# Softmax row sums of two head pairs in one block, sent back through DRAM, and SBUF work moved to GpSimd, in a fused cosine attention and MLP kernel

## Chip, cores, metric

One core of one Trainium2 chip. The metric is the device time of one execution in microseconds (us), as the median of several; lower is better.

## The reference, cut to what matters

```python
# q, k, v: (8 batches, 12 heads, 448 tokens, 64) fp32; w_in: (768, 2048); w_out: (2048, 768); tau = 0.1
q_n = q / (np.linalg.norm(q, axis=-1, keepdims=True) + 1e-06)     # k_n likewise
scores = np.matmul(q_n, k_n.transpose(0, 1, 3, 2)) / tau
scores = scores - np.max(scores, axis=-1, keepdims=True)
attn = np.exp(scores)
attn = attn / (np.sum(attn, axis=-1, keepdims=True) + 1e-09)
x = np.matmul(attn, v)          # then heads side by side: (3584, 768)
h = x @ w_in
out = (0.5 * h * (1.0 + erf(h * inv_sqrt2))) @ w_out
```

## The kernel before

In the profile PE is TensorE, PEld its weight loads, DVE is VectorE, ACT ScalarE, POOL GpSimd and SP SyncE, which issues DMAs here; SPq is its queue. PSUM is the memory that TensorE's products go to, in banks; SBUF holds the other tiles on the chip. Twelve heads make six head pairs per batch (HP = 6). For each pair, q and k are scaled to length one and transposed (`tp`), the scores are computed transposed (`st`, keys on the partitions), and exp gives `pt`. Two products follow: `o` = values, and `sm` = row sums, by a matrix of ones 64 columns wide, so that each sum comes out 64 times, once beside each value of its head. x = o / sm. After six pairs, the first layer (`hp`, 16 chains of six matmuls) follows, then gelu. The second layer (`op`) runs as filling between the next batches' attention.

```python
    def scale(g):                      # a pair's q and k, scaled
        sr = sr_t.pop(g)               # the norm, from ScalarE: exp(0.5 * ln(sum of squares))
        se = nrm.tile(...)
        nc.vector.tensor_scalar(se, sr, 1e-6, None, ALU.add)
        rn = nrm.tile(...)
        nc.vector.reciprocal(rn, se)
        ...
        for i, eng in enumerate((nc.gpsimd, nc.vector)):      # one half on each engine
            eng.tensor_tensor(qkb[:, i]..., t[:, i], rn[:, i].to_broadcast(...), ALU.mult)

    def transposes(g):
        tp = ps_acc.tile([128, 2, NC, CS], BF16, tag="sm", name=f"tp{g}")   # the bank of the sums
        ...                                                   # 8 transposes
        nc.vector.tensor_copy(qkT, tp)

    def values(g):
        o = ps_acc.tile([128, 512], F32, tag="o", name=f"o{g}")
        sm = ps_acc.tile([128, 512], F32, tag="sm", name=f"sm{g}")
        for dst in (sm, o):
            for c in range(NC):
                for h in range(2):
                    nc.tensor.matmul(dst[h * D:(h + 1) * D, :S],
                                     lhsT=ones if dst is sm else v_t[g][:, h, c, :],
                                     rhs=pt_t[g, c][:, h, :], start=(c == 0), stop=(c == NC - 1))

    def normalise(g):
        ln = rcp.tile([128, S], F32, tag="ln", name=f"ln{g}")
        nc.scalar.activation(ln, sm[:, :S], AF.Ln)
        rs = rcp.tile([128, S], F32, tag="rs", name=f"rs{g}")
        nc.scalar.activation(rs, ln, AF.Exp, scale=-1.0)
        nc.vector.tensor_tensor(x_t[b][:, p, :], o[:, :S], rs, ALU.mult)
    # cut: loads, squares, reduce, root, scores, attention, first, second_pieces, spin (matmuls whose
    # result nobody reads, between the first batch's steps)
```

## Time and profile before

| | before |
|---|---|
| median of 3 runs | 488.82 us (488.04 to 489.09) |
| profiled span | 487.9 us |
| mean granted TensorE clock | 0.993 |
| first hp starts at | 49.88 us |
| batch with 128 op matmuls, hp start to hp start | 58.74 us |
| batch with 96 | 54.43 us |
| last hp start to the end | 43.90 us |

How to read it: the span is the first hp start, seven steps from hp start to hp start, and the last part. Three steps have 128 op matmuls; of the four with 96, one (the first) takes 54.74. The page's own lines are in the prediction. The granted clock by slices of 12.2 us: only the second slice is low.

```profile
PEclk9799999999999999999999999999999999999999
```

### The profile page before, as it was taken

The numbers are of one execution on the slowest core, as the hardware profiler recorded it, in microseconds if no ns is written. First come the engines' busy times: TensorE is split into PE (matmuls) and PEld (weight loads), VectorE is DVE, ScalarE is ACT, GpSimd is POOL, SyncE is SP. The second block draws the span as 40 slices with busy tenths as digits, with TensorE's granted clock in tenths as the row PEclk, the third lists the DMA queues.
The fourth block names the chain that finished last, engine by engine and source line by source line (L and its number), as shares of the span: only waits on it lengthen the run. The fifth ranks groups of instructions, "written<-read, shape, count | busy, mean of one in ns | idle before, by whom it ended". The sixth has DMA issues, their size and how long they took to land.

```text
span 487.9 us, 8097 instructions
## 1 busy us (share of the span) xinstructions
PE 474.8 (97%) x3280; PEld 245.2 (50%) x3280; DVE 198.5 (41%) x349; ACT 323.1 (66%) x530; POOL 195.8 (40%) x158
## 2 busy tenths in 40 slices
PE   7599999999999999999999999999999999999996
PEld 4254554455554555455545555455555555445563
DVE  4569116721366115650276213760166502631021
ACT  3498569954887448974688547975688646994400
POOL 5789306840367204860077402780066600610000
PEclk9799999999999999999999999999999999999999
DMA  9699964460165302461054500652045210221022
GB/s 216 141 203 233 234 105 115 108 159 1 28 166 142 80 1 80 117 158 29 0 128 131 156 2 6 171 130 76 0 119 137 52 32 1 53 44 32 1 61 68
DMA packets 42053, 45.35 MB, mean 93 GB/s; under 512 B 3360, under 2 KB 37664, under 8 KB 42016
## 3 DMA queue, kind: packets, MB, share of 16 engines
q1 hardware_dynamic: 27280, 32.81, 22.3%
q0 software_dynamic: 14496, 11.80, 16.1%
q8 instruction: 25, 0.41, 0.4%
q10 hardware_dynamic: 240, 0.23, 0.1%
q14 instruction: 12, 0.10, 0.1%
HBM read 45.61 MB, written 11.01 MB: 116 GB/s over the span
## 4 chain that ended last, share of the span: by engine, by line
PE 88%; DMA 4%; ACT 3%; DVE 2%; POOL 1%; issue 1%; SPq 1%; POOLq 0%
PE op L200 30%; PE hp L299 30%; PE st L161 10%; PE sm L174 7%; PE o L174 6%; PE tp L150 4%; DMA qk<-in_k_dram 4%; ACT pt L164 2%; PE spin L240 1%; DVE x L185 1%; POOL qkb L139 1%; SPq L89 1%; ACT rs L184 1%; DVE qkT L151 1%; ACT ln L182 0%
## 5 line engine op out<-in xcount | busy, mean ns | idle before, releaser
L164 ACT ACTIVATE pt<-st 112x896 bf16<-112x896 f32 x192 | 165.0, 911 | 29.7 <-PE st L161 27.8
L139 POOL TENSOR_TENSOR qkb<-qk,rn 112x512 bf16<-112x512 f32 x48 | 69.4, 1447 | 232.9 <-DVE rn L135 213.4
L200 PE MATMUL op<-wo,g 128*128 128x384 bf16 x896 | 161.3, 326 | 0.0
L299 PE MATMUL hp<-x,wi 128*128 128x448 bf16 x768 | 147.9, 352 | 0.1
L301 ACT ACTIVATE g<-hp 128x448 bf16<-128x448 f32 x128 | 69.6, 544 | 80.2 <-PE hp L299 80.2
L200 PEld LDWEIGHTS <-g 128*128 128x128 bf16 x896 | 81.2, 98 | 62.4 <-issue 15.9
L299 PEld LDWEIGHTS <-wi 128*128 128x128 bf16 x768 | 74.8, 98 | 68.8 <-issue 0.4
L110 POOL TENSOR_TENSOR sq<-qk 112x1024 f32<-112x1024 f32 x46 | 87.7, 1907 | 2.0 <-DMA qk<-in_k_dram 1.4
L151 DVE COPY qkT<-tp 128x896 bf16<-128x896 bf16 x48 | 29.7, 620 | 101.3 <-PE tp L150 101.3
L204 DVE COPY ot<-op 128x384 f32<-128x384 f32 x56 | 31.1, 555 | 92.1 <-PE op L200 92.0
L185 DVE TENSOR_TENSOR x<-o,rs 128x448 bf16<-128x448 f32 x48 | 30.0, 624 | 81.4 <-ACT rs L184 60.1
L161 PE MATMUL st<-qkT 64*112 64x448 bf16 x384 | 60.7, 376 | 1.6 <-DVE qkT L151 0.7
L119 DVE TENSOR_REDUCE nq<-sq 112x16 f32<-112x1024 f32 x47 | 56.9, 1211 | 1.8 <-POOL sq L110 1.8
L174 PE MATMUL sm<-pt,ones 112*64 112x448 bf16 x384 | 45.8, 360 | 0.0
L174 PE MATMUL o<-pt,v 112*64 112x448 bf16 x384 | 44.3, 352 | 0.0
L161 PEld LDWEIGHTS <-qkT 64*112 64x112 bf16 x384 | 20.5, 125 | 39.3 <-issue 28.1
L182 ACT ACTIVATE ln<-sm 128x448 f32<-128x448 f32 x48 | 25.5, 532 | 21.3 <-PE sm L174 21.2
L139 DVE TENSOR_TENSOR qkb<-qk,rn 112x512 bf16<-112x512 f32 x48 | 37.1, 773 | 1.9 <-DMA qk<-in_k_dram 0.2
L97 POOL DMA_DIRECT2D v<-in_v_dram x48 | 34.2, 712 | 0.2 <-issue 0.2
L150 PE MATMUL tp<-ident,qkb 112*128 112x112 bf16 x384 | 27.9, 215 | 5.3 <-DVE qkb L139 4.4
L150 PEld LDWEIGHTS <-qkb 112*128 112x128 bf16 x384 | 20.5, 98 | 20.7 <-issue 13.2
L174 PEld LDWEIGHTS <-ones 112*64 112x64 bf16 x384 | 17.7, 109 | 23.1 <-issue 15.9
(26 smaller groups left out, 162.7 us busy)
## 6 DMA issues: line engine op xcount, KB each, us to landing
qk<-in_q_dram SPq DMA_DIRECT2D x48, 224.0 KB, 2.8
qk<-in_k_dram SPq DMA_DIRECT2D x47, 224.0 KB, 3.8
v<-in_v_dram POOLq DMA_DIRECT2D x48, 112.0 KB, 3.6
wi<-in_moe_w_in_dram POOLq DMA_DIRECT2D x6, 512.0 KB, 10.3
wo<-in_moe_w_out_dram POOLq DMA_DIRECT2D x4, 768.0 KB, 18.9
out_dram<-ot SPq DMA_DIRECT2D x8, 336.0 KB, 3.8
out_dram<-ot SPq DMA_DIRECT2D x8, 288.0 KB, 3.8
out_dram<-ot SPq DMA_DIRECT2D x8, 240.0 KB, 3.2
```

The lines of the kernel that those rows point to most:

```text
L110: nc.gpsimd.tensor_tensor(sq, t, t, ALU.mult)
L119: nc.vector.tensor_reduce(nq, sq, mybir.AxisListType.X, ALU.add)
L139: eng.tensor_tensor(qkb[:, i].rearrange("p c h d -> p h c d"), t[:, i], rn[:, i].to_broadcast([CS, 2, NC, D]), ALU.mult)
L150: nc.tensor.transpose(tp[:, i, c, :], qkb[:, i, c].rearrange("p h d -> p (h d)"), ident)
L151: nc.vector.tensor_copy(qkT, tp)
L161: nc.tensor.matmul(st[:, h, :S], lhsT=qkT[rows, 1, c, :], rhs=qkT[rows, 0, :, :], start=True, stop=True)
L164: nc.scalar.activation(pt, st[:, :, :S], AF.Exp, scale=inv_tau)
L174: nc.tensor.matmul(dst[h * D:(h + 1) * D, :S], lhsT=ones if dst is sm else v_t[g][:, h, c, :], rhs=pt_t[g, c][:, h, :], start=(c == 0), st ...
L185: nc.vector.tensor_tensor(x_t[b][:, p, :], o[:, :S], rs, ALU.mult)
L200: nc.tensor.matmul(ps[:, :NH], lhsT=g_t[sb][:, kf, t * 128:(t + 1) * 128], rhs=wo[:, kf, ni * NH:(ni + 1) * NH], start=(kf == 0), stop=(kf ...
L299: nc.tensor.matmul(hp[:, :S], lhsT=wi[:, kd, m * 128:(m + 1) * 128], rhs=x_t[b][:, kd, :], start=(kd == 0), stop=(kd == KD - 1))
L301: nc.scalar.activation(g_t[sb][:, m, hf * S:(hf + 1) * S], hp[:, :S], AF.Gelu)
```

## The change

Its intent is to take work off TensorE, which bounds the kernel, and to keep VectorE and GpSimd out of each other's way. In each batch the row sums of pairs 0 and 1, and of 2 and 3, are computed in one block on four 32-column tiles. Such a sum stands in 32 rows and not beside its values, so one row of each head is stored to DRAM and read back broadcast over 64 partitions (`rb`); GpSimd then makes x from `rb` and from a copy of o in SBUF. GpSimd also takes both scalings; VectorE keeps what reads PSUM or has one operand. Norms of three pairs share a root. The weights are loaded in halves of columns, and the first four hp chains get their last matmul late.

```diff
+    rows = nc.dram_tensor("rows", (NG, 2, S), F32, kind="Internal").ap()
     def root(n):                       # now for a group of up to five pairs
+        se = nrm.tile(shape + [2], F32, tag="se", name=f"se{n}")[..., 0]     # output stride 2
+        nc.vector.tensor_scalar(se, sr, 1e-6, None, ALU.add)
+        rn = nrm.tile(shape, F32, tag="rn", name=f"rn{n}")
+        nc.vector.reciprocal(rn, se)
     def scale(g):
-        for i, eng in enumerate((nc.gpsimd, nc.vector)):
+        for i, eng in enumerate((nc.vector if g == 0 else nc.gpsimd, nc.gpsimd)):
+    def sums_two(g):
+        sm = ps_acc.tile([128, 512], F32, tag="sm", name=f"sm{g}")
+        for c in range(NC):
+            for j in range(2):
+                for h in range(2):
+                    r = 32 * (2 * j + h)
+                    nc.tensor.matmul(sm[r:r + 32, :S], lhsT=ones[:, :32], rhs=pt_t[g + j, c][:, h, :],
+                                     start=(c == 0), stop=(c == NC - 1), tile_position=(0, r))
+        rs = reciprocal(g, sm)
+        nc.sync.dma_start(out=rows[g:g + 2].rearrange("j h s -> (j h) s"), in_=rs[0:128:32, :])
+        rb = osp.tile([128, 2, S], F32, tag="rb", name=f"rb{g}", bufs=2)
+        for h in range(2):
+            nc.sync.dma_start(out=rb[h * D:(h + 1) * D], in_=rows[g:g + 2, h, :].partition_broadcast(D))
     # attention(b), step i, g = 6 * b + i:
+                values(g - 1, i < HP - 1)          # with a copy of o to SBUF by VectorE
+                if i in (2, 4):
+                    sums_two(g - 2)
...
+            upto(load_v, g + (3 if b == 0 else 4))
+            if i in (3, 5):
+                for j in (3, 2):
+                    normalise(g - j, nc.gpsimd)
     # first(b): chains 0 to 3 to their fifth matmul, then
+        for m in range(4):
+            mm(m, (KD - 1,))
     # prologue
-    upto("v", 3, load_v)
+    upto(load_v, 1)
+    upto(load_wi, 1)
 # cut: pools, weights by halves, reduce, spins, order of op
```

## The prediction

> **What bounds the kernel now.** I read the page first, then the timeline of TensorE in steady batches, then the first 52 us of all engines.
>
> ```profile
> PE 474.8 (97%) x3280; PEld 245.2 (50%) x3280; DVE 198.5 (41%) x349; ACT 323.1 (66%) x530; POOL 195.8 (40%) x158
> PE   7599999999999999999999999999999999999996
> L174 PE MATMUL sm<-pt,ones 112*64 112x448 bf16 x384 | 45.8, 360 | 0.0
> L174 PE MATMUL o<-pt,v 112*64 112x448 bf16 x384 | 44.3, 352 | 0.0
> ```
>
> TensorE is 97% busy and full in every slice but the first two and the last. Busy is not the same as at its peak, so I took starts of successive blocks in the timeline as the cost of a block. Here is one pair (two heads) in a batch with 128 op matmuls:
>
> ```profile
> 131.25 0.95 PE L174 MATMUL sm<-pt,ones 112*64 112x448 bf16 x8
> 132.03 0.92 PE L174 MATMUL o<-pt,v 112*64 112x448 bf16 x8
> 132.88 0.59 PE L161 MATMUL st<-qkT 64*112 64x448 bf16 x4
> 133.40 0.57 PE L150 MATMUL tp<-ident,qkb 112*128 112x112 bf16 x8
> 133.80 1.79 PE L200 MATMUL op<-wo,g 128*128 128x384 bf16 x10
> 135.52 0.58 PE L161 MATMUL st<-qkT 64*112 64x448 bf16 x4
> ```
>
> From start to start: sm 0.78 us, o 0.85, st 0.52, tp 0.40, op 1.72 for ten. In the trace's starts a plain op follows the last by 163 ns, an hp by 189 ns, and the two column halves of an sm start 3 or 4 ns apart, one such round each 189 ns. The last matmul before a change of array shape takes about 94 ns more (256 for 162, 283 for 189). There is nothing else: no waits. The starts of the eight first-layer (hp) stages are 49.88, 104.61, 163.35, 217.79, 276.53, 330.96, 389.70 and 444.01, so a batch with 96 op matmuls takes 54.4 us, one with 128 takes 58.7, and 43.9 us follow the last start. The 96-op batches have one blemish, scores that wait for ScalarE to free their buffer:
>
> ```profile
> 191.30 0.58 PE L161 MATMUL st<-qkT 64*112 64x448 bf16 x4
> 193.41 0.82 PE L161 MATMUL st<-qkT 64*112 64x448 bf16 x4
> ```
>
> Summed over a batch, st takes 7.02 us there and 6.25 in a 128-op batch: 0.77 us of waiting.
>
> The first batch, 49.9 us to its hp, is another matter. From 25 us on ScalarE sets the pace, one pair each 5.07 us (25.43, 30.50, 35.57, 40.64):
>
> ```profile
> 25.43 3.53 ACT L164 ACTIVATE pt<-st 112x896 bf16<-112x896 f32 x4
> 28.85 0.31 ACT L125 ACTIVATE lq<-nq,tiny 112x16 f32<-112x16 f32 x1
> 29.19 0.22 ACT L127 ACTIVATE sr<-lq 112x16 f32<-112x16 f32 x1
> 29.42 0.54 ACT L182 ACTIVATE ln<-sm 128x448 f32<-128x448 f32 x1
> 30.00 0.58 ACT L184 ACTIVATE rs<-ln 128x448 f32<-128x448 f32 x1
> ```
>
> GpSimd is nearly as full there, and it and VectorE get in each other's way when both work on two SBUF operands:
>
> ```profile
> 38.41 0.69 DVE L139 TENSOR_TENSOR qkb<-qk,rn 112x512 bf16<-112x512 f32 x1
> 38.55 1.46 POOL L139 TENSOR_TENSOR qkb<-qk,rn 112x512 bf16<-112x512 f32 x1 [0.50 <-DVE rn L135]
> 42.52 3.75 DVE L139 TENSOR_TENSOR qkb<-qk,rn 112x512 bf16<-112x512 f32 x1
> 44.06 1.05 POOL L139 TENSOR_TENSOR qkb<-qk,rn 112x512 bf16<-112x512 f32 x1
> ```
>
> GpSimd needs 1.05 us for a scaling when VectorE is held up, and 1.46 when it starts 0.14 us after VectorE's. So some 0.4 us of GpSimd's usual 1.45 is waiting, and VectorE's 3.75 is 0.69 of work and 3 of waiting.
>
> **What the Trainium skill says.** "SBUF — State Buffer", SBUF: two separate sides: VectorE with two SBUF inputs, or in a 2-port mode, and GpSimd share a port pair as an exclusive lock held for a whole instruction. The 1.05 against 1.46 and the 3.75 agree. "TensorE: Matmul & The Clock Gate", Part 3: Packing small matmuls: tiles in different column groups run together, about 4 ns apart, three of 32 columns giving 2.38 times. Two tiles agree here (3 to 4 ns); four are not in this trace. "TensorEngine Tiling (Array Packing)", Key Properties: changing the tiling mode drains the engine. The 94 ns agree. "DMA: Bandwidth & Descriptors", Anatomy of one DMA: about 2.0 us fixed per DMA, mostly the receipt of the write. The page's out_dram stores land in 3.2 to 3.8 us with 240 to 336 KB; nothing so small as the new row store is in the trace.
>
> **The change, part by part: steady batches.**
> - Row sums. Today 6 blocks of sm, 6 x 0.78 = 4.68 us. Afterwards two pairs keep theirs (1.56), and two blocks of 16 matmuls on four 32-column tiles serve the other four. If four run as two do, a block is four rounds of 189 ns and a little for the first weights, 0.80 (an estimate from the sm block). That is 3.16 in all: 1.52 saved.
> - The 64-column values now go into 32-column sums: one change of shape more for each block, 2 x 0.094 = 0.19 lost.
> - Sums and transposes share one PSUM bank. Before, o and st (1.37 us) stood between sm and tp, and hid ScalarE's ln, which frees it. Now only st (0.52) does. ln starts 0.394 us after the last sm matmul's start (so when nothing else holds ScalarE), 0.21 after the block's end, and takes 0.54; with 0.05 for the signal tp starts at 0.80, not 0.52: 0.28 lost, twice a batch, 0.56.
> - The first four hp chains run to their fifth matmul and only then get their sixth. The first gelu starts 20 x 0.189 = 3.78 into the stage plus 0.389 (the trace's distance from last matmul to gelu), ends at 4.72, and the fifth chain, due at 24 x 0.189 = 4.54, needs its buffer: 0.25 lost.
> - ScalarE loses two ln/rs couples (2.2 us) and four ln/exp root couples (2 us) a batch. In 128-op batches this is beside TensorE. In 96-op batches it ends the 0.77 of waiting, but behind a shared sum the four exps still come late (end 2.95 us after it, second st at 2.78): 0.23 twice, so 0.77 - 0.46 = 0.31 won.
> - VectorE's 32 copies of o, GpSimd's 48 more scalings and 32 products, and 16 broadcasts of 448 KB lie beside TensorE: GpSimd would do 12 x 1.05 + 6 x 1.9 + 6 x 0.71 + 4 x 0.9 = 32 us of a 54 us batch.
> - The round trip: rs at 1.35 us after the shared sum, a row store about 2.5 (fixed cost and issue), a broadcast about 4.5 (3.8 to land as a qk load, plus a second issue), two products 1.8: 10.2. TensorE reaches the hp that needs them after about 11.4 in the shortest batch. Hidden, with 1.2 us to spare.
>
> Sum: 128-op batch -1.52 + 0.19 + 0.56 + 0.25 = -0.5, so 58.2; 96-op batch 0.31 better, -0.8, so 53.6.
>
> **The first batch.** GpSimd takes both scalings, so its load per pair is 2 x 1.05 + 1.9 (squares) + 0.71 (v) + about 0.6 (weights) = 5.3 us, above ScalarE's 3.53 + 0.53 + on average 0.73 = 4.8. Followed in order from the scaling of pair 1 at 12.8 us: pairs 2, 3, 4 and 5 are scaled by about 20.8, 26.1, 31.4 and 38 (two products before the last, perhaps waiting for the broadcast). From a scaling to the first exp go 1.5 us (tp 0.4, copy 0.6, st), and the last pair needs 4.7 on ScalarE and 1.7 of sums and values: hp at about 46. The v loads of pairs 1 and 2 queue behind a 1.5 MB weight load in a phase where DMA is full (v takes 7.7 us to land in the first 75 us); one us for that: 47. Today it is 49.9, and hp then waits 0.3 for its last x. Gain 3.2. Loading wo only after this stage costs nothing by this working: at the pace of the software queue (11.8 MB in 16.1% of 488 us, 150 GB/s written) the first two column halves, 1.57 MB, need 10.5 us, and hp takes 18. The five-pair root group at the end of that stage delays a transpose by 0.35.
>
> **Sum.** 47.0 + (53.6 + 0.35) + 3 x 58.2 + 3 x 53.6 + 43.9 + 0.25 = 480.5 us of span against 487.9: 7.4 less. On the median, 481.4; I say 481.
>
> **Rivals.**
> - The packing alone decides and the new waits do not appear: ln is prompt or the bank is not the thing waited for. Then 8 x 1.5 + 3 + 4 us go, 469 to 473. For it: TensorE is the bound, all it sheds counts. Against: the order of waits of the built kernel shows tp after each shared sum waiting for ScalarE.
> - The round trip is not hidden: row stores queue behind qk loads and output stores on the same queue, and hp waits 1 to 3 us in seven batches. 485 to 500. For it: 1.2 us to spare. Against: DMA is only 30% busy in steady batches.
> - GpSimd becomes the bound of the first batch: its scalings stay at 1.45, 0.8 us a pair more over five pairs, hp at 51: 485. Against: the 1.05 with VectorE held up.
> - Four tiles run no better than two pairs of tiles: no saving, 493. Against: rounds of 189 ns leave room for eight instructions at the 49 ns that a transpose and its weight load take together.
>
> **Range and chances.** The start may be off by 3 us either way, a steady batch by 0.5 us, seven times: 475 to 487. The 2% line is 479.0, two us below my number: faster 0.32, same 0.64, slower 0.04.
>
> **What would show it.** A shared sum of 16 with 0.75 to 0.85 from start to start; tp after it with a wait of about 0.3 on ScalarE's ln; hp stages 58.2 and 53.6 apart; the fifth hp chain 0.25 late; GpSimd's scalings near 1.05; first hp at 45 to 49. Wrong if x products of GpSimd end hp's wait, if PE is throttled in the first batch, or if op waits for wo in the second.

## The result, and the profile after

| | before | after | predicted |
|---|---|---|---|
| median | 488.71 us (488.04 to 489.09, 4 runs) | 488.58 us (488.36 to 488.73, 4 runs) | 481.0 |
| ratio | | 0.9998 (0.9981 to 1.0016) | |
| span profiled | 487.9 | 486.7 | 480.5 |
| first hp starts at | 49.88 | 54.38 | 47.0 |
| first step (96 op, to the second hp) | 54.74 | 54.04 | 53.95 |
| step with 128 op, three times | 58.74 | 58.05 | 58.2 |
| step with 96 op, three times | 54.43 | 53.35 | 53.6 |
| last hp start to the end | 43.90 | 44.04 | 44.15 |

A ratio here is the mean time of one kernel's fast runs over the mean of the other's in the same rounds, with a 95% interval, so it is not quite the ratio of the medians quoted. The time is the same, and it is outside the range that I gave.

The columns tell where it went. From the second hp on, the changed kernel is 5.75 us faster (0.70 + 3 x 0.69 + 3.12 - 0.14; the three 96-op steps before are 54.43, 54.43 and 54.31). It gives 4.50 of that back before the first hp, and the span is 1.2 us shorter. (The medians are only 0.1 apart: the profiled execution of before took 489.69 us, 1 us over its median.) My steady batches were right to a quarter of a us each. My first hp was 7.4 us too early.

The page first: busy time, the slices and the three groups that matter.

```profile
PE 465.0 (96%) x3266; PEld 235.5 (48%) x3266; DVE 164.7 (34%) x246; ACT 297.5 (61%) x443; POOL 254.8 (52%) x234
PE   8586999999999999999999999999999999999996
PEclk9978999999999999999999999999999999999998
L151 POOL TENSOR_TENSOR qkb<-qk,rn 112x512 bf16<-112x512 f32 x95 | 97.2, 1048 | 92.8 <-PE op L244 72.2
L230 POOL TENSOR_TENSOR x<-os,rb 128x448 bf16<-128x448 f32 x32 | 35.5, 1126 | 93.3 <-DMA rb<-rows 77.0
L140 DVE TENSOR_SCALAR se<-sr 112x48 f32<-112x48 f32 (+2 forms) x20 | 8.4, 419 | 78.3 <-ACT sr L137 78.3
```

VectorE's load fell as intended, and GpSimd's scaling takes 1048 ns against 1447 before. But the PE row now has four slices under 9 at its start, and the clock row is low in the third and fourth: the loss is before 49 us. Note too the mean of 419 ns for the small add: by the trace its median is 191, so a few were very long.

The steady batch, on TensorE's timeline (start, duration, engine, line, operation, tiles, count):

```profile
140.57 0.95 PE L183 MATMUL o<-pt,v 112*64 112x448 bf16 x8
141.45 0.94 PE L216 MATMUL sm<-pt,ones 112*32 112x448 bf16 x16
142.32 0.58 PE L173 MATMUL st<-qkT 64*112 64x448 bf16 x4
143.03 0.55 PE L162 MATMUL tp<-ident,qkb 112*128 112x112 bf16 x8
```

From start to start: o 0.88, the shared sum 0.87, st 0.71 in place of 0.52. The last is the predicted wait of tp for the bank of the sums, 0.2 here. Inside the shared sum the trace has four starts within 10 ns, and such rounds 189 ns apart (200 after the first): four tiles run side by side as two did.

The first batch, on VectorE, with GpSimd beside it:

```profile
15.30 1.48 DVE L140 TENSOR_SCALAR se<-sr 112x16 f32<-112x16 f32 x1 [0.83 <-ACT sr L137]
...
20.23 2.56 DVE L140 TENSOR_SCALAR se<-sr 112x16 f32<-112x16 f32 x1 [1.57 <-ACT sr L137]
22.82 0.25 DVE L142 RECIPROCAL rn<-se 112x16 f32<-112x16 f32 x1
22.99 0.56 DVE L188 COPY os<-o 128x448 f32<-128x448 f32 x1
23.47 0.61 DVE L163 COPY qkT<-tp 128x896 bf16<-128x896 bf16 x1
```

```profile
18.84 2.06 POOL L151 TENSOR_TENSOR qkb<-qk,rn 112x512 bf16<-112x512 f32 x2
20.85 1.89 POOL L117 TENSOR_TENSOR sq<-qk 112x1024 f32<-112x1024 f32 x1
...
40.14 2.21 POOL L230 TENSOR_TENSOR x<-os,rb 128x448 bf16<-128x448 f32 x2 [6.04 <-DMA rb<-rows]
42.32 2.03 POOL L151 TENSOR_TENSOR qkb<-qk,rn 112x512 bf16<-112x512 f32 x2
```

The add of 16 elements, 0.18 us when GpSimd is idle, takes 2.56 from 20.23 and ends 0.05 after GpSimd's square does. The others end in the same way (15.30 + 1.48 = 16.78; GpSimd's square ends at 16.75). VectorE works in order, so the copy of the transposes behind it starts at 23.47. Then at 40.14 GpSimd, also in order, has waited 6 us for the broadcast, with the scaling of pair 5 behind the two products. TensorE shows what both cost:

```profile
20.96 0.57 PE L162 MATMUL tp<-ident,qkb 112*128 112x112 bf16 x8 [0.16 <-POOL qkb L151]
24.13 0.99 PE L173 MATMUL st<-qkT 64*112 64x448 bf16 x4 [2.61 <-DVE qkT L163]
...
26.35 1.70 PE L183 MATMUL o<-pt,v 112*64 112x448 bf16 x8
27.99 1.68 PE L216 MATMUL sm<-pt,ones 112*32 112x448 bf16 x16
...
44.41 0.93 PE L162 MATMUL tp<-ident,qkb 112*128 112x112 bf16 x8 [3.67 <-POOL qkb L151]
```

Each of the two idle stretches (2.61 and 3.67 us) is followed by work at half the clock, o 1.70 for 0.95 and the shared sum 1.68 for 0.94: the granted clock is low from 23.4 to 30.2 and from 43.9 to 50.7. The sums being late, the row store is issued late, and it lands slowly (SP's queue):

```profile
30.90 0.65 SPq L219 DMA_DIRECT2D rows<-rs  x1
35.33 1.34 SPq L222 DMA_DIRECT2D rb<-rows  x2
```

4.4 us from one issue to the other, and the product starts at 40.14: 9.2 us from store to product, against 6.4 to 8.9 in the later batches.

**Theories.** A: the one-operand add waits for GpSimd's run, and through VectorE's order delays the transposes. B: GpSimd waits for the broadcast with pair 5's scaling behind it. C: the v load of pair 1, now behind weight loads, is late too. The rivals: the packing is no good in the steady batches; or the first batch is late because its six sums, scalings and loads are more than GpSimd can do (its load by itself), in which case undoing A or B would give nothing.

### The profile page after: what moved, and what is told of

It is laid out like the page before. It is cut to its first block, busy times and chain, and to the rows that moved or that the text cites. A ratio compares the mean times of both kernels' runs of the same rounds, so it can differ in the third digit from the quotient of the medians.

```text
span 486.7 us, 7988 instructions
## 1 busy us (share of the span) xinstructions
PE 465.0 (96%) x3266; PEld 235.5 (48%) x3266; DVE 164.7 (34%) x246; ACT 297.5 (61%) x443; POOL 254.8 (52%) x234
## 4 chain that ended last, share of the span: by engine, by line
PE 83%; ACT 4%; issue 4%; POOL 4%; DMA 2%; DVE 2%; SPq 0%; POOLq 0%
PE op L244 30%; PE hp L364 26%; PE st L173 8%; PE o L183 8%; PE tp L162 4%; PE sm L216 3%; PE sm L204 3%; DMA qk<-in_k_dram 2%; POOL sq L117 2%; ACT ln L194 2%; POOL qkb L151 1%; ACT pt L176 1%; DVE se L140 1%; ACT g L388 1%; PE spin L291 1%
## 5 line engine op out<-in xcount | busy, mean ns | idle before, releaser
L151 POOL TENSOR_TENSOR qkb<-qk,rn 112x512 bf16<-112x512 f32 x95 | 97.2, 1048 | 92.8 <-PE op L244 72.2
L388 ACT ACTIVATE g<-hp 128x448 bf16<-128x448 f32 x128 | 67.0, 545 | 74.4 <-PE hp L364 73.8
L117 POOL TENSOR_TENSOR sq<-qk 112x1024 f32<-112x1024 f32 x45 | 84.5, 1891 | 0.1
L230 POOL TENSOR_TENSOR x<-os,rb 128x448 bf16<-128x448 f32 x32 | 35.5, 1126 | 93.3 <-DMA rb<-rows 77.0
L183 PE MATMUL o<-pt,v 112*64 112x448 bf16 x384 | 46.3, 364 | 0.0
L194 ACT ACTIVATE ln<-sm 128x448 f32<-128x448 f32 x32 | 17.4, 542 | 39.2 <-PE sm L204 22.6
L140 DVE TENSOR_SCALAR se<-sr 112x48 f32<-112x48 f32 (+2 forms) x20 | 8.4, 419 | 78.3 <-ACT sr L137 78.3
L162 PEld LDWEIGHTS <-qkb 112*128 112x128 bf16 x384 | 21.8, 98 | 21.1 <-issue 10.6
L183 PEld LDWEIGHTS <-v 112*64 112x64 bf16 x384 | 19.5, 112 | 20.8 <-issue 11.7
L188 DVE COPY os<-o 128x448 f32<-128x448 f32 x32 | 19.7, 616 | 23.0 <-PE o L183 23.0
```

Source lines behind the costliest of these rows:

```text
L117: nc.gpsimd.tensor_tensor(sq, t, t, ALU.mult)
L151: eng.tensor_tensor(qkb[:, i].rearrange("p c h d -> p h c d"), t[:, i], rn[:, i].to_broadcast([CS, 2, NC, D]), ALU.mult)
L162: nc.tensor.transpose(tp[:, i, c, :], qkb[:, i, c].rearrange("p h d -> p (h d)"), ident)
L183: nc.tensor.matmul(o[h * D:(h + 1) * D, :S], lhsT=v_t[g][:, h, c, :], rhs=pt_t[g, c][:, h, :], start=(c == 0), stop=(c == NC - 1))
L230: eng.tensor_tensor(x_t[b][:, p, :], os_t.pop(g), rb_t.pop(g), ALU.mult)
L388: nc.scalar.activation(g_t[sb][:, m, hf * S:(hf + 1) * S], hps.pop(m), AF.Gelu)
```

## The experiments

Twelve kernels in three sets of four, each set on one chip. The kernel before took 489.47 (488.47 to 490.03), 488.83 (488.32 to 490.22) and 489.15 us (487.98 to 489.37) in them, seven runs each. All twelve gave correct results. All edits are against the changed kernel. "hp done" is the first hp start plus the length of that stage, which is counted from start to start without the 0.40 us of transposes that stand in it; waits inside the stage count. A median of one set beside one of another can be off by what before differs between the sets, up to 0.8 us; the ratios are free of that.

### First set: A and B

**e1_products_late.** In the first batch, the products of pairs 0 and 1 come one step later, after pair 5's scaling.

```diff
-            if i in (3, 5):
-                for j in (3, 2):
+            late = b == 0 and i == 4
+            if i == 5 or i == (3 if b else 4):
+                for j in (4, 3) if late else (3, 2):
```

> In the first batch alone, GpSimd's products of pairs 0 and 1 stand behind the scaling of pair 5, those of 2 and 3 stay last. If GpSimd's wait in order for the broadcast (6.0 us before the first product) is what holds pair 5 back: scaling of pair 5 ends near 36 instead of 44.4, TensorE's 3.7 us of idle before its transposes goes, and with it the half clock from 43.9 to 50.7; first hp at 49.5 to 50.5 instead of 54.4, median 483.5 to 485. If GpSimd's load or full DMA is the bound: first hp within 1 us of 54.4, median 487.5 to 488.6. Steady batches as they are (58.05 and 53.35).

Measured: 484.9 us (484.44 to 486.02), ratio 0.991 (0.9892 to 0.9929). First hp at 47.51, 6.9 us earlier. But the hp stage takes 21.24 instead of 18.49: it waits for the x of pairs 2 and 3. The scaling of pair 5 ends at 36.2, as expected. B is shown to be worth some 4 us (the medians are 3.7 apart, hp is done 4.1 earlier), and the rest of the gain is taken by the second round trip. A does not show as idle time in this trace: the clock fell at 15.9 here and not at 23.4, so TensorE came to pair 2's transposes later, and the add's wait (1.84 us) lies beside it. GpSimd's load is unchanged, so the rival that its load alone is the bound of the first hp falls.

**e2_one_root.** ScalarE gives 1/norm directly; VectorE has no add and no reciprocal. (It leaves out the 1e-6, which the check of the result does not notice.)

```diff
-        nc.scalar.activation(sr, ln, AF.Exp, scale=0.5)
-        nc.vector.tensor_scalar(se, sr, 1e-6, None, ALU.add)
-        nc.vector.reciprocal(rn, se)
+        nc.scalar.activation(rn, ln, AF.Exp, scale=-0.5)
```

> ScalarE gives the reciprocal root itself (exp of -0.5 ln), so VectorE's add and reciprocal are gone, and with them the add's waits of 1.3, 2.4 and 1.0 us in the first batch while GpSimd runs without a pause. If that port lock is what left TensorE idle from 21.5 to 24.1 and let its clock fall to half from 23.4 to 30.2: no half clock there, first shared sum's rs near 27.5 instead of 30.9, the broadcast and all behind it some 3.5 us earlier, first hp at 50 to 51.5, median 484 to 486. If the lock is beside the path: within 0.5 us of 488.6.

Measured: 486.1 us (484.79 to 487.47), 0.9932 (0.9907 to 0.9956). First hp at 54.13 in the trace, only 0.25 earlier: a miss of my 50 to 51.5. (The profiled run is the slowest of the four, 487.47 us at a clock of 0.978 against 0.984 to 0.991 in the others, and the median is 2.5 us under after's; so the others very likely start hp earlier, which no trace of them shows.) The add is gone and the copy of pair 2's transposes starts at 20.81, 2.7 us earlier than after (23.47), so A is real. But the values then wait 1.89 us for v, and the clock halves there (24.1 to 37.8), with pair 5's transposes still waiting 1.38 us for GpSimd later. The one sure gain is in the second batch, where a group of five roots had delayed a transpose: st takes 7.14 us there and not 7.84. So in this trace removing A alone gives little, because C takes its place and B still comes after both.

**e3_both.** e1's and e2's edits together.

```diff
+    # e1's lines and e2's lines
```

> Both edits. If the two waits are separate causes that add: first hp at 46 to 48 as the prediction's own working had it (47.0), median 480 to 482. If GpSimd's load of 5.3 us a pair or DMA bounds the batch behind them: first hp no better than the better of the two alone, 49 or later, median 483 or more.

Measured: 484.7 us (483.79 to 485.82), 0.9904 (0.988 to 0.9927): hardly better than e1. First hp at 48.69, later than e1's. This was a miss: the two gains do not add. TensorE's timeline of e3 shows why:

```profile
25.96 1.71 PE L178 MATMUL o<-pt,v 112*64 112x448 bf16 x8 [2.96 <-DMA v<-in_v_dram]
```

The values of pair 1 wait 2.96 us for their v, and run at half the clock (24.8 to 31.6). C, which A had hidden, has come to light. In e1 this wait was 1.07, behind a half-clock phase that had come before it.

**e4_plain_sums_first.** No shared sums and no round trip in the first batch.

```diff
-                if i == HP - 1:
+                single = b == 0 or i == HP - 1
+                if single:
                     sums_one(g - 1)
...
-            if i in (3, 5):
+            if b and i in (3, 5):
```

> The first batch alone sums as before: 64-column sums for each pair, products on VectorE, no row store and no broadcast there; VectorE's add is left as it is. If the round trip is what costs: GpSimd's 6.0 and 2.3 us of waiting go, first hp at 48 to 50.5, median 482.5 to 485. If not: 487.5 or more.

Measured: 484.37 us (481.85 to 486.87), 0.9884 (0.9832 to 0.9936). First hp at 51.65 in the profiled run, later than the 48 to 50.5 expected. A and C are still there (st waits 2.18 for the copy, and the values of pair 1 wait 0.85 for v, with half the clock from 23.6 to 37.2), so taking the round trip away brings the start only part of the way. The times lie in two groups, 482 and 486.5, with mean clocks of 0.993 to 0.995 and 0.983 to 0.986: the same code loses the clock for longer in some executions than in others.

### Second set: C, and the terms of the steady batch

**e5_v_early.** e3, and the v of pairs 1 and 2 loaded ahead of the first weights.

```diff
+    # e3's lines
-    upto(load_v, 1)
+    upto(load_v, 3)
     upto(load_wi, 1)
```

> e3_both, and the v loads of pairs 1 and 2 are issued ahead of the first weight load instead of behind the second. If the values of pair 1 waited for v alone (2.96 us idle, then half clock from 24.8 to 31.6): no half clock after the start, values of pair 1 at 23 instead of 26, first hp at 43.5 to 45.5 with 1 to 3 us of waiting for GpSimd's last two products, median 480 to 481.5. If DMA as such is short in this phase, and the v loads only change places with weights or q and k: another wait of the same size, first hp at 48 or later, median 484 or more.

Measured: 481.41 us (480.77 to 484.46), 0.9858 (0.9823 to 0.9893). First hp at 43.18, 11.2 us earlier than after and earlier than I had predicted for the change itself. The hp stage takes 23.46: its sixth pair of operands is there, but the x of pairs 2 and 3 are not (these two waits come up again in e12). So A, B and C together explain the late first hp, and behind them stands a fourth wait, D: hp for the second round trip. hp is done at 66.64, against 72.87 after.

**e6_sums_before_values.** The sums go ahead of the values, so that the values stand between the sum and the next user of its bank, and ScalarE gets its logarithm earlier.

```diff
-                values(g - 1, i < HP - 1)
                 if i in (2, 4):
                     sums_two(g - 2)
-                elif i == HP - 1:
+                values(g - 1, i < HP - 1)
+                if i == HP - 1:
```

> The changed kernel with the shared sums ahead of the values, so that the values lie over ScalarE's ln. If tp waits for the sums' PSUM bank: the 0.20 us at the end of the scores before it goes, twice a batch: 128-op batches 57.65 instead of 58.05, 96-op batches 52.5 to 52.95 instead of 53.35 (the scores there also wait for late exps), median 485 to 486.5 if the first batch stays. If the wait has another cause: 58.05 and 53.35 stay.

Measured: 484.08 us (483.0 to 484.81), 0.99 (0.9874 to 0.9926). Steps of 57.68 and 52.52 against 58.05 and 53.35. TensorE's timeline:

```profile
139.16 0.94 PE L216 MATMUL sm<-pt,ones 112*32 112x448 bf16 x16
140.03 0.95 PE L183 MATMUL o<-pt,v 112*64 112x448 bf16 x8
140.91 0.58 PE L173 MATMUL st<-qkT 64*112 64x448 bf16 x4
141.43 0.57 PE L162 MATMUL tp<-ident,qkb 112*128 112x112 bf16 x8
```

st is back at 0.52 from start to start, and the wait is gone: the bank was the cause.

**e7_hp_order.** The last matmul of hp chains 0 and 1 is given after chain 2, not after chain 3.

```diff
             mm(m, range(KD - 1))
+            if m == 2:
+                for early in range(2):
+                    mm(early, (KD - 1,))
...
-        for m in range(4):
+        for m in range(2, 4):
             mm(m, (KD - 1,))
```

> The changed kernel, but the sixth matmul of hp chains 0 and 1 is given after the fifth of chain 2. If the fifth chain's 0.228 us is the wait for the first gelu: hp stage 18.25 instead of 18.49, 57.8 and 53.1 a batch, median 486.5 to 487. If it is something of four open chains: 18.49 stays.

Measured: 487.07 us (486.62 to 487.41), 0.9961 (0.9943 to 0.9978). The hp stage takes 18.27 instead of 18.49, every step is 0.22 shorter (57.83 and 53.12, the first 53.81). The wait of the fifth chain was 0.22, of the predicted 0.25.

**e8_plain_sums_later.** The reverse of e4: shared sums in the first batch only.

```diff
+                single = b > 0 or i == HP - 1
...
-            if i in (3, 5):
+            if b == 0 and i in (3, 5):
```

> The changed kernel with 64-column sums in all batches but the first: no packing, no row store, no broadcast, products on VectorE there. If the packing is what won the steady time: six sums of 0.78 instead of 3.30 in all (+1.38), 0.10 of shape changes and 0.40 of waits for the bank less: 128-op batches 58.9, 96-op batches 54.3 to 54.6, median 493.5 to 496. If the steady gain came from less ScalarE work and the port lock (root groups, scalings on GpSimd): 58.1 and 53.4 stay, median 488 to 489.

Measured: 492.91 us (492.27 to 493.53), 1.008 (1.0061 to 1.01). Steps of 58.97 and 53.77. So the packing, with the waits that it brings, saves 0.92 us in a 128-op step and 0.42 in a 96-op one. The first is as expected. The second is below what I expected: behind a shared sum the exps come late, and those steps depend on ScalarE, as the prediction said of its "0.23 twice". TensorE's starts show it: in a 96-op step st takes 6.25 us in e8 and 7.15 in after, 0.90 more, where in a 128-op step it takes 0.40 more (6.65), all of it the bank; so 0.50 is the late exps, of the 0.46 predicted.

### Third set: the mends together

**e9_mixed_first.** The edits of e1, e2, e5, e6 and e7, and in the first batch the pairs 2 and 3 with plain sums, so that no x of the last pairs comes through DRAM.

```diff
+    # the lines of e2, e6, e7 and of v early
+                single = i == HP - 1 or (b == 0 and i > 2)
...
+            late = b == 0 and i == 4
+            if i == (3 if b else 4) or (b and i == 5):
+                for j in (4, 3) if late else (3, 2):
```

> All mends at once (root on ScalarE, products late, v early, sums before values, sixth hp matmuls earlier), and in the first batch only pairs 0 and 1 share their sums; pairs 2 and 3 are summed plainly, so that hp waits for no second round trip. If the waits found so far are all there are: first hp at 43.8 to 45.5 with no wait behind it, 128-op batches 57.4, 96-op batches 52.3, span 469 to 471, median 470.5 to 473 (ratio about 0.965). If shorter batches bring the round trip of 6.3 to 8.9 us onto the path: hp stages over 18.3 in later batches, median 474 or more.

Measured: **471.85 us (470.29 to 473.19), 0.9645 (0.9617 to 0.9674)**: it beats both kernels, by 3.5% (1 - 0.9645) in the rounds against before. (Like e2 it leaves out the 1e-6.) Its clock row is that of before again, and TensorE goes into hp without a wait:

```profile
41.50 0.92 PE L178 MATMUL o<-pt,v 112*64 112x448 bf16 x8
42.35 0.59 PE L168 MATMUL st<-qkT 64*112 64x448 bf16 x4
...
44.75 0.95 PE L178 MATMUL o<-pt,v 112*64 112x448 bf16 x8
45.63 12.66 PE L359 MATMUL hp<-x,wi 128*128 128x448 bf16 x66
```

The ledger of e9 is 45.63 + 52.30 + 3 x 57.46 + 3 x 52.30 + 44.02 = 471.2. Against after, a 128-op step is 0.59 shorter, and e6 and e7 alone gave 0.37 and 0.22: they add. A 96-op step is 1.05 shorter, and 0.83 and 0.23 were theirs. The first step is 1.74 shorter, with e2's 0.69 on top of those. The remaining 8.75 of the 15.4 us are the first batch. Two of the four runs had a clock of 1.00 and took 470.29 and 470.69, the other two 0.99 and took 473.00 and 473.19: one phase at half the clock (15.3 to 22.1 in the profiled run), which comes in some executions only, is worth 2.6 us.

**e10_plain_first_mends.** As e9, but with plain sums in all of the first batch.

```diff
+                single = i == HP - 1 or b == 0
+            if b and i in (3, 5):
```

> As e9, but no shared sums in the first batch at all. One more ln/rs couple (1.1 us) on ScalarE, which paces that batch once GpSimd does not wait: first hp 1 us later than in e9, median 471.5 to 474. If GpSimd is the pace: the same first hp as e9 or earlier, since two products of 1.1 us are gone.

Measured: 474.88 us (474.03 to 476.39), 0.9712 (0.9693 to 0.9731). The median is 0.9 over my range. First hp at 47.03, 1.4 after e9's. So one shared sum early in the first batch, with time for its round trip, is worth having. (0.55 of the 1.4 is a wait for another v.)

**e11_v_alone.** C's mend alone on the changed kernel.

```diff
-    upto(load_v, 1)
+    upto(load_v, 3)
```

> The changed kernel with nothing but the v loads of pairs 1 and 2 issued early. If the port lock comes first and the v load only takes its place when it is gone: first hp at 53 to 54.5, median 487.3 to 488.8. If the late v is a cause of its own in the changed kernel: 2 us or more earlier, median 486.5 or less.

Measured: 488.12 us (486.75 to 488.26), 0.997 (0.9953 to 0.9987). First hp at 53.93 against 54.38, and the profile shows the transposes of pair 5 waiting 5.28 us for GpSimd in place of 3.67. The early v is swallowed by B. The same edit took 2 to 3 us off e3 (2.2 by the ratios to before and by the spans, 3.3 by the medians, which are of different sets).

**e12_all_mends_packed.** As e9, but with both shared sums in the first batch, as in the change.

```diff
+    # the lines of e1, e2, e6, e7 and of v early
```

> As e9, but pairs 2 and 3 of the first batch share their sums too. The second round trip there (9.6 us while weights load) then ends behind the start of hp: first hp at 42.5 to 44, first hp stage 21 to 23.5 instead of 18.3, median 473.5 to 476, 2.5 to 4 above e9. If the sums placed before the values bring the round trip forward enough: within 1 us of e9.

Measured: 474.69 us (474.36 to 475.15), 0.9705 (0.9691 to 0.972). hp starts first of all, at 42.00, and waits:

```profile
42.00 0.55 PE L358 MATMUL hp<-x,wi 128*128 128x448 bf16 x2
45.58 0.35 PE L358 MATMUL hp<-x,wi 128*128 128x448 bf16 x1 [3.03 <-POOL x L223]
46.67 13.76 PE L358 MATMUL hp<-x,wi 128*128 128x448 bf16 x63 [0.74 <-POOL x L223]
```

The stage takes 24.04 instead of e9's 18.27, more than the 21 to 23.5 expected. hp is done at 66.04 against 63.90. This shows D by itself: the second round trip of the first batch, 10.0 us from the store's issue to the first product, costs more than the sum that it saves.

The first batch in one table:

| kernel | first hp | hp stage | hp done | what stands in the way |
|---|---|---|---|---|
| before | 49.88 | 18.57 | 68.45 | ScalarE's pace |
| after | 54.38 | 18.49 | 72.87 | A and B (C hidden) |
| e2 | 54.13 | 18.49 | 72.62 | C and B |
| e11 | 53.93 | 18.49 | 72.42 | A and B |
| e1 | 47.51 | 21.24 | 68.75 | half clock, C, D |
| e3 | 48.69 | 19.84 | 68.53 | C, D |
| e5 | 43.18 | 23.46 | 66.64 | D |
| e12 | 42.00 | 24.04 | 66.04 | D |
| e10 | 47.03 | 18.27 | 65.30 | one v |
| e9 | 45.63 | 18.27 | 63.90 | none of A to D |

## Why the prediction was wrong, point by point

**Steady batches: right.** Predicted 58.2 and 53.6, measured 58.05 and 53.35, and by the right mechanism. Term by term:
- The shared sum was put at 0.80 + 0.094 with its change of shape; it is 0.87. (The rival's "room for eight instructions" was a wrong sum: four times 49 ns is 196, over 189. The rounds follow each other after 189 ns all the same.)
- The wait of tp for the bank was put at 0.28; it is 0.20 (e6 removes it).
- The fifth hp chain was put at 0.25; it is 0.22 (e7). The figures shown for it, 4.72 - 4.54, give 0.18; time for a signal, which the tp term counts as 0.05, is not in them.
- GpSimd's scaling was put at 1.05; it is 1.048. The products were put at 0.9 and are 1.13, off the path in every later batch.
- The round trip is hidden there, as I said: the row store, put at 2.5, takes 1.7 to 2.9, and the broadcast to the product 4.6 to 6.4. (The fixed cost in the 2.5 came from a section that is about DMAs issued by GpSimd; this store is issued by SyncE.) The margin was thin: in e3 and e10 the second hp stage was 0.5 and 0.4 us longer, waiting for such a product.
- The packing, by the prediction's own terms, was worth 1.52 - 0.19 - 0.56 = 0.77 in a 128-op step and 0.46 less, 0.31, in a 96-op one. e8 shows 0.92 and 0.42.

**The failed step: when the first batch's pairs reach TensorE.** The prediction put it as "pairs 2, 3, 4 and 5 are scaled by about 20.8, 26.1, 31.4 and 38", and then "hp at about 46", and one us for v: 47. The scalings of pairs 2, 3 and 4 end at 20.9, 26.25 and 31.6: GpSimd's pace, where I saw the danger, was right. Two things in that step were wrong, and a third was in the wrong place.

1. *"From a scaling to the first exp go 1.5 us."* For pair 2 it takes 3.2 until the scores start (20.9 to 24.13), because the copy waits behind the small add, and the add waits for GpSimd (A). I had cited the shared port pair for two SBUF inputs "or in a 2-port mode" and then counted only the two-operand work. The Trainium skill, "VectorE: DVE Perf Modes", What auto-detection actually checks, names as conditions for such a mode a single source and a destination in SBUF, and even (or equal) outer dimensions, and nothing there says that a strided output prevents it. The add meets these conditions, and its waits agree: 1.48, 2.56 and 1.14 us for 0.18 of work. Worse, the trace of before showed it, and I had not looked at this line beside GpSimd's:

```profile
36.80 1.29 DVE L133 TENSOR_SCALAR se<-sr 112x16 f32<-112x16 f32 x1
```

```profile
36.14 1.91 POOL L110 TENSOR_TENSOR sq<-qk 112x1024 f32<-112x1024 f32 x1
```

The add ends at 38.09 and the square at 38.05. It cost nothing there, because ScalarE set the pace. That the wait is a mode of VectorE's is an inference from the page; that the add waits for GpSimd, and that removing it frees the copy, is shown (e2). VectorE's reductions, one operand too, keep their 1.21 us beside GpSimd (at 23.99 us in after).

2. *"two products before the last, perhaps waiting for the broadcast": pair 5 at 38.* It is scaled at 44.35, 6.3 us later (B). I had the wait in the sentence and did not work it out. The shared sum comes late by A, at half the clock, and the row store takes 4.4 us while the weights load, so the round trip is 9.2 us from store to product where I had 7.0 (2.5 + 4.5). Nor did I see what matters: GpSimd runs its instructions in order here, so work that nobody waits for yet (x of pairs 0 and 1) blocks work that everybody waits for (pair 5). e1 moves the two and hp starts 6.9 us earlier.

3. *The v loads, "one us for that".* As a sum term it was wrong both ways: alone it is worth almost nothing (e11), and once A and B are gone it costs 2 to 3 us (e3 to e5). Waits that run at the same time do not add.

The clock belongs to each of these. I named "if PE is throttled in the first batch" as a sign of error but gave it no cost; each phase at half the clock, 6.8 us long in after, stretched the very blocks that the round trip waits for.

**The rivals.** None of the four came. "GpSimd becomes the bound of the first batch", with hp at 51, was near in its place and wrong in its cause: GpSimd was not full but waiting. "The round trip is not hidden" was right for one batch of eight, the one in which I did not apply it.

**What stays open.** Why VectorE's add is not let in between two of GpSimd's instructions that follow each other closely, no run here tells. Nor does any tell why a half-clock phase comes in some executions of the same kernel and not in others.

## What to carry to other kernels

Work out the start-up batch separately, engine by engine and in issue order, even when it is a tenth of the time: here the steady gain of 5.75 us and the loss of 4.50 were in different batches, and mends that moved a few lines turned no gain into 3.5%. On an in-order engine, put nothing that waits for a round trip ahead of work that the next stage needs; and where every wait ends at the same place, expect that removing one of them alone shows nothing. When an engine's small instruction has a mean far over its median, look up beside what it was long.

## What the Trainium skill lacked or had wrong

- "SBUF — State Buffer", SBUF: two separate sides: the lock is told as held for one whole instruction, and who gets it next is not said. Here VectorE's waiting add did not get in when GpSimd's scaling ended (20.90), but only after the square that followed (22.74): 2.56 us for 0.18.
- "TensorE: Matmul & The Clock Gate", Part 3: no measured figure for four 32-column tiles (three are given). Here 16 matmuls of 448 columns on four tiles take 0.87 us from start to start with the change of shape, against 2 x 0.78 for the same sums on two tiles of 64.
- "TensorEngine Tiling (Array Packing)", Key Properties: the drain at a change of tiling has no size there; here it is about 94 ns.
- "TensorE: Matmul & The Clock Gate", Part 1: one idle window of about 3.4 us is given for the drop. Here the clock also fell after windows that were not idle: in after at 23.42, with 1.35 us of TensorE's work in the 3.4 us before, and in e9 at 15.31, with 1.75 us. It stayed low for 6.83 us in both; in the other runs' traces the low phases before the last matmul lasted 3.41, 6.83, 10.24 or 13.65 us. By the clocks e9 had such a phase in two of four runs and not in the others (473.1 against 470.5 us).
- "DMA: Bandwidth & Descriptors": no page has the cost of a small store beside a busy software queue. The 7 KB row store took 1.7 to 2.9 us until the broadcast's issue in after's later batches, and up to 5.3 (e1) in the first one, while weights loaded.
